# Hash attention by whole pairs: scores of both query halves in one phase, hashes, values and sums in another

## Chip, cores, metric

One core of a Trainium2 chip runs the kernel. The metric is the device time of one execution in microseconds (us), median over runs. Ratios are the mean time of one kernel's runs over the mean of the other's runs of the same rounds, so they are not quite the ratio of the medians that stand beside them.

## The reference

```python
def _attn_ref(q, k, v, proj):              # 4 x 8 heads, 768 tokens, head size 64
    q_bucket = sum(((q @ proj) > 0) * 2**arange(6))      # k_bucket likewise
    mask = q_bucket[:, :, :, None] == k_bucket[:, :, None, :]
    scores = where(mask, q @ k.T / 8, -1e9)
    attn = exp(scores - max) / (sum + 1e-9)
    return attn @ v
def _moe_ref(x, w_in, w_out):              # 3072 x 512, 512 x 2048, 2048 x 512
    h = x @ w_in
    return (h * sigmoid(1.702 * h)) @ w_out
```

The attention's output, laid out as 3072 x 512, is the input of the second block. All is float32. The change touches the attention stage alone, about the first 325 us.

## The kernel before

Attention goes over 16 pairs of heads (n = 0 to 15). The 768 queries of a pair are two halves (c = 0, 1). For each half and each of six key tiles TensorE computes scores into PSUM, ScalarE takes the exponential into SBUF (`es[c]`), GpSimd adds the exponentials of tiles 0 to 2 (`add_low`), VectorE those of tiles 3 to 5 and GpSimd's result (`add_high`), and TensorE multiplies all six with the values. Around this lie the hashes of the next pair, the row totals `dn` of the pair before, and the normalization. VectorE also converts a piece of `w_in` per pair, in the steps of `convert`.

The lines are shortened, and the loop is shown as it runs for pairs 1 to 15.

```python
def turn(n, name):                         # qT or kT of pair n: a VectorE transpose (L391)
    nc.vector.transpose(xt, x)
def hashed(n):                             # TensorE, L408: k and q, both halves, four column tiles
def featured(n):                           # VectorE f (L413), then 8 small DMAs to feats
def add_low(n, c):                         # GpSimd, L440 and L441
    acc = accs[n, c, 0] = st.tile(..., tag="acc0", bufs=1)
    nc.gpsimd.tensor_tensor(acc, es[c][:, 0], es[c][:, 1], op=Alu.add)
    nc.gpsimd.tensor_tensor(acc, acc, es[c][:, 2], op=Alu.add)
def add_high(n, c):                        # VectorE, L446, L448, L448
    nc.vector.scalar_tensor_tensor(acc, e[0], T * TINY, e[1], op0=Alu.add, op1=Alu.add)
    for x in (e[2], accs.pop((n, c, 0))):
        nc.vector.tensor_tensor(acc, acc, x, op=Alu.add)
def total(n):                              # TensorE, L479: dn, in PSUM pool mps
def invert(n):                             # VectorE: rt from dn, reciprocals r, rs
def norm(n):                               # VectorE, L499: xT times rs, two SBUF inputs
... (cut)
for g in range(len(groups) + 2):           # a group is one half (n, c)
    scores(n, c, kts); add_low(n, c)
    if hashes: featured(hashes.pop())
    if ended: add_high(*prev[:2])          # prev is the group before
    ... (turn k, norm, total of the pair before, turn q, invert)
    values(*prev); unload(*prev[:2])
    if "q" in turned: hashed(n + 1); fetch(n + 2, "k"); fetch(n + 2, "q"); fetch_v(n + 1)
    step(n, 3)                             # three conversion steps
```

So TensorE's order in a pair is scores, dn, values, hashes, scores, values: a half's values run one group after its scores.

## Time and profile before

| | kernel before |
|---|---|
| time, median | 878.85 us (878.79 to 879.34) |
| TensorE busy | 99% of the span |
| VectorE busy | 82% of the span; in attention 0.75 us idle per pair |
| one pair of attention | 19.53 us (the last two that can be counted: 19.99 and 19.97) |
| granted TensorE clock, mean (1 is full speed) | 0.997 |

The page and the chain that ended last tell what bounds the kernel; the chain in order of time shows of what a pair consists; the timelines of VectorE and GpSimd show what happens beside it. The lines are in the prediction.

### The profile page before, as it was taken

How to read it: one execution, taken by the hardware profiler on the slowest of the kernel's cores; microseconds unless marked ns; L12 is line 12 of the kernel's file. 1: busy time of each engine (PE TensorE's matmuls, PEld its weight loads, DVE VectorE, ACT ScalarE, POOL GpSimd, SP SyncE). 2: the span in 40 equal slices, each digit the busy share in tenths (PEclk: the TensorE clock that was granted, in tenths of full speed). 3: DMA queues.
4: the chain of work that ended last, by engine and by line, in shares of the span. 5: the costliest groups of instructions: out<-in, count | busy, mean ns of one | idle time of the engine just before them, and what ended most of it. 6: DMA issues, size and time to landing. Idle time of an engine off the chain costs nothing.

```text
span 877.2 us, 11895 instructions
## 1 busy us (share of the span) xinstructions
PE 866.8 (99%) x4077; PEld 498.4 (57%) x4077; DVE 723.3 (82%) x1020; ACT 314.8 (36%) x519; POOL 323.7 (37%) x275
## 2 busy tenths in 40 slices
PE   9999999999999999999999999999999999999996
PEld 5444444444444444444444444444888888888885
DVE  4589989999999986787777887888897977897786
ACT  5766776677666642223232223322000000000000
POOL 4343343333433364675433444559903100000000
PEclk9999999999999999999999999999999999999998
DMA  5544545665544203555455545575845685477524
GB/s 131 94 63 82 106 83 93 100 99 91 83 83 85 67 1 133 203 204 192 160 195 208 201 164 199 184 250 179 309 155 182 188 230 210 157 221 241 192 96 100
DMA packets 169157, 132.01 MB, mean 150 GB/s; under 512 B 123616, under 2 KB 138112, under 8 KB 163712
## 3 DMA queue, kind: packets, MB, share of 16 engines
q1 hardware_dynamic: 166528, 129.70, 52.1%
q10 hardware_dynamic: 2560, 1.46, 0.7%
q8 instruction: 34, 0.56, 0.3%
q14 instruction: 35, 0.29, 0.1%
HBM read 79.69 MB, written 50.33 MB: 148 GB/s over the span
## 4 chain that ended last, share of the span: by engine, by line
PE 97%; DVE 2%; DMA 0%; issue 0%; ACTq 0%; ACT 0%; DVEq 0%
PE product L708 33%; PE product L820 27%; PE ps L432 18%; PE av L458 15%; PE dn L479 2%; PE hash L408 1%; DVE xT L824 1%; PE tp L366 1%; DVE y L800 1%; DMA k<-in_k_dram 0%; PE hash L373 0%; DVE v L824 0%; DVE t2a L221 0%; DVE raw_g L220 0%; ACTq L807 0%
## 5 line engine op out<-in xcount | busy, mean ns | idle before, releaser
L433 ACT ACTIVATE e<-ps 128x768 f32<-128x768 f32 x192 | 151.2, 812 | 15.0 <-PE ps L432 12.7
L432 PE MATMUL ps<-qT,kT 64*128 64x384 f32 x768 | 155.1, 482 | 0.0
L708 PE MATMUL product<-xT,w_in_sb 128*128 128x512 f32 x288 | 135.5, 593 | 0.0
L458 PE MATMUL av<-e,v 128*64 128x385 f32 x768 | 131.5, 490 | 0.0
L440 POOL TENSOR_TENSOR acc<-e 128x768 f32<-128x768 f32 x32 | 58.7, 1835 | 192.5 <-DVE acc L448 130.1
L716 ACT ACTIVATE c<-c 128x512 f32<-128x512 f32 x72 | 45.4, 630 | 186.8 <-issue 78.9
L458 PEld LDWEIGHTS av<-e,v 128*64 128x64 f32 x768 | 52.2, 136 | 76.4 <-issue 75.9
L708 PEld LDWEIGHTS product<-xT,w_in_sb 128*128 128x128 f32 x288 | 54.6, 190 | 69.2 <-issue 64.1
L708 PE MATMUL product<-t_x,s_in 128*128 128x512 f32 x192 | 90.2, 592 | 0.0
L432 PEld LDWEIGHTS ps<-qT,kT 64*128 64x128 f32 x768 | 68.1, 188 | 35.4 <-issue 35.3
L219 POOL TENSOR_TENSOR v<-c,u 128x512 f32<-128x512 f32 x24 | 34.2, 1425 | 123.2 <-ACT c L716 123.2
L833 ACT COPY u<-product 128x256 f32<-128x256 f32 x21 | 7.8, 373 | 172.1 <-PE product L820 138.9
L432 PE MATMUL ps<-qf,kf 64*128 64x384 bf16 x384 | 62.9, 324 | 0.1
L708 PEld LDWEIGHTS product<-t_x,s_in 128*128 128x128 f32 x192 | 36.5, 190 | 45.9 <-issue 43.8
L441 POOL TENSOR_TENSOR acc<-acc,e 128x768 f32<-128x768 f32 x32 | 59.1, 1847 | 2.5
L708 PE MATMUL product<-xT,s_in 128*128 128x512 f32 x96 | 45.1, 592 | 0.0
L708 PE MATMUL product<-t_x,w_in_sb 128*128 128x512 f32 x96 | 45.1, 592 | 0.0
L432 PEld LDWEIGHTS <-kf 64*128 64x128 bf16 x384 | 18.9, 94 | 41.3 <-issue 19.5
L446 DVE SCALAR_TENSOR_TENSOR acc<-e 128x768 f32<-128x768 f32 x32 | 32.2, 1007 | 5.1 <-ACT e L433 5.1
L469 ACT COPY vs<-av 128x1 f32<-128x1 f32 x32 | 5.1, 159 | 86.1 <-PE av L458 86.1
L820 PE MATMUL product<-raw_g,xT 128*128 128x256 f32 x152 | 35.1, 379 | 0.0
L448 DVE TENSOR_TENSOR acc<-acc,e 128x768 f32<-128x768 f32 x32 | 32.3, 1009 | 3.3
(207 smaller groups left out, 1546.3 us busy)
## 6 DMA issues: line engine op xcount, KB each, us to landing
raw_g<-g_dram SPq DMA_DIRECT2D x22, 1024.0 KB
s_in<-g_dram SPq DMA_DIRECT2D x20, 1024.0 KB
g_dram<-c SPq DMA_DIRECT2D x72, 256.0 KB
g_dram<-t SPq DMA_DIRECT2D x48, 256.0 KB
raw<-in_moe_w_in_dram SPq DMA_DIRECT2D x16, 512.0 KB
raw<-in_moe_w_out_dram SPq DMA_DIRECT2D x16, 512.0 KB
v<-in_v_dram SPq DMA_DIRECT2D x32, 192.0 KB
g_dram<-u SPq DMA_DIRECT2D x24, 256.0 KB
```

The source lines that it names most:

```text
L219: return [lambda: eng.tensor_tensor(t1, b12, b11, op=Alu.subtract), lambda: eng.tensor_tensor(b12, b22, b12, op=Alu.subtract), lambda: eng ...
L432: nc.tensor.matmul(ps[:, j, 0:HS], a[hs, keys], m[hs, cols], start=not last, stop=last)
L433: nc.scalar.activation(es[c][:, kt, :, 0:HS], ps[:, :, 0:HS], Act.Exp, scale=1.0 / D**0.5)
L440: nc.gpsimd.tensor_tensor(acc, es[c][:, 0, :, 0:HS], es[c][:, 1, :, 0:HS], op=Alu.add)
L441: nc.gpsimd.tensor_tensor(acc, acc, es[c][:, 2, :, 0:HS], op=Alu.add)
L446: nc.vector.scalar_tensor_tensor(acc, e[0], T * TINY, e[1], op0=Alu.add, op1=Alu.add)
L448: nc.vector.tensor_tensor(acc, acc, x, op=Alu.add)
L458: nc.tensor.matmul(av[D * j : D * (j + 1), :], vt[:, t, j, :], es[c][:, t, j, :], start=(t == 0), stop=(t == T - 1))
L479: nc.tensor.matmul(dn[r0 : r0 + 32, :], ones[:, 0:32], acc[:, j, :], start=True, stop=True)
L708: nc.tensor.matmul(ps, wq[LEFT[i]][:, kc, :], xq[RIGHT[i]][:, kc, :], start=(kc == 0), stop=(kc == K2 - 1))
L716: nc.scalar.activation(c, c, Act.Gelu_apprx_sigmoid)
L820: nc.tensor.matmul(ps, wq[LEFT[i]][:, c, :], gq[RIGHT[i]][:, c, :], start=(c == 0), stop=(c == F4 - 1))
```

## The change

The intent: run both halves' scores in one go and both halves' values in one go, so that TensorE changes its tile shape less often. The loop over groups becomes a loop over pairs. The core of the diff (pairs 1 to 15; pair 0 is written out, and is much as before):

```diff
-pool, tag = (mps, "m") if (n, c) == (last, 1) else (aps, "av")
+pool, tag = (mps, "m") if c else (aps, "av")
-dn = accs[n] = mps.tile([P, HS], F32, tag="m", name="dn")
+dn = accs[n] = aps.tile([P, HS], F32, tag="av", name="dn")
-for g in range(len(groups) + 2):
-    ... (cut)
+for n in range(1, last + 1):
+    scores(n, 0, every)
+    add_low(n, 0)
+    if n == 1:
+        add_high(0, 1)
+        turn(2, "k")
+        total(0)
+    invert(n - 1)
+    norm(n - 1)
+    if 1 < n < last:
+        turn(n + 1, "k")
+    scores(n, 1, every)
+    add_low(n, 1)
+    add_high(n, 0)
+    if n < last:
+        turn(n + 1, "q")
+        hashed(n + 1)
+        featured(n + 1)
+        ... (measure; in the last pair two guards instead)
+    step(n, 2)
+    add_high(n, 1)
+    values(n, 0, every)
+    unload(n, 0)
+    step(n, 4)
+    values(n, 1, every)
+    unload(n, 1)
+    total(n)
+    ... (fetches of n + 2, conversion and sums)
```

More of the change, by code (lines that the diff above doesn't have):

```diff
@@ L485, in invert @@
                 nc.vector.transpose(rt.rearrange("p s i -> p (s i)"), accs.pop(n))
-                yield
                 r = st.tile([P, 2, HS // 32], F32, tag="r", name="r")
@@ L499, in norm @@
                 nc.vector.tensor_tensor(x, x, rs.rearrange("p (t s) -> p t s", t=T), op=Alu.mult)
-            groups = [(n, c, kts) for n in range(len(pairs)) for c in range(2)
-                      for kts in ((range(GT), range(GT, T)) if n == 0 else (range(T),))]
             last = len(pairs) - 1
@@ L525, in guard @@
                     nc.vector.tensor_reduce(largest[0:1, 0:1], row, axis=AX.X, op=Alu.max)
-            totals, norms, hashes = [], [], []
+            low, high, every = range(GT), range(GT, T), range(T)
             rest = first_pair()
@@ L532, in attention @@
                 fetch(1, x)
-            for g in range(len(groups) + 2):
-                n, c, kts = groups[g] if g < len(groups) else (last + 1, 0, ())
-                prev = groups[g - 1] if 1 <= g <= len(groups) else None
-                if kts:
-                    scores(n, c, kts)
-                    if g == 0:
-                        rest()
-                    if kts[0] == 0:
-                        add_low(n, c)
-                if hashes:
-                    featured(hashes.pop())
-                ended = prev and prev[2][-1] == T - 1
-                if ended:
-                    add_high(*prev[:2])
-                    if prev[1] == 1:
-                        totals.append((g + (g == len(groups)), prev[0]))
-                turned = ("", "k", "q", "")[g] if n == 0 else "kq" if c == 0 and n < last else ""
-                inverted = iter(())
-                for x in turned[:1]:
-                    turn(n + 1, x)
-                    measure(n + 1, x)
-                while norms:
-                    norm(norms.pop(0))
-                if totals and totals[0][0] == g:
-                    norms.append(totals.pop(0)[1])
-                    total(norms[-1])
-                    inverted = invert(norms[-1])
-                    next(inverted)
-                for x in turned[1:]:
-                    turn(n + 1, x)
-                    measure(n + 1, x)
-                whole(inverted)
-                if prev:
-                    values(*prev)
-                if ended:
-                    unload(*prev[:2])
-                if "q" in turned:
-                    hashed(n + 1)
-                    if n:
-                        hashes.append(n + 1)
-                    else:
-                        featured(n + 1)
-                    for x in "kq" if n else "q":
-                        if n + 2 <= last:
-                            fetch(n + 2, x)
-                    fetch_v(n + 1)
-                elif turned:
-                    fetch(n + 2, turned)
-                if kts and kts[-1] == T - 1:
-                    step(n, 3)
-                    if c == 0 and n > last - len(x_sums):
-                        x_sums[n - last - 1]()
-                    if c == 1:
-                        begin(n + 1)
-                if g in (len(groups) - 3, len(groups) - 2):
-                    guard(g - len(groups) + 3)
-                if g == len(groups):
-                    for f in in_sums(0):
-                        f()
-                    early.close()
-                    next(ff)
@@ L598, in attention @@
-            for x in norms:
-                norm(x)
+            scores(0, 0, low)
+            rest()
+            add_low(0, 0)
+            scores(0, 0, high)
+            turn(1, "k")
+            measure(1, "k")
+            values(0, 0, low)
+            fetch(2, "k")
+            scores(0, 1, low)
+            add_low(0, 1)
+            add_high(0, 0)
+            turn(1, "q")
+            measure(1, "q")
+            values(0, 0, high)
+            unload(0, 0)
+            hashed(1)
+            featured(1)
@@ new lines, in attention @@
+            fetch(2, "q")
+            fetch_v(1)
+            scores(0, 1, high)
+            values(0, 1, low)
+            values(0, 1, high)
+            unload(0, 1)
+            for n in range(1, last + 1):
[14 more added lines that the diff above has]
+                    turn(n + 1, "q")
+                    hashed(n + 1)
+                    featured(n + 1)
+                    for x in "kq":
+                        measure(n + 1, x)
+                else:
+                    guard(0)
+                    guard(1)
+                step(n, 2)
[6 more added lines that the diff above has]
+                total(n)
+                if n + 2 <= last:
+                    for x in "kq":
+                        fetch(n + 2, x)
+                if n < last:
+                    fetch_v(n + 1)
+                    begin(n + 1)
+                if n > last - len(x_sums):
+                    x_sums[n - last - 1]()
@@ L602, in shifted_attention @@
+            for f in in_sums(0):
+                f()
+            early.close()
+            next(ff)
+            invert(last)
+            norm(last)
     def shifted_attention():
```

## The prediction

> **What bounds the kernel now.** I read the page first: engine totals, then the chain that ended last.
>
> ```profile
> PE 866.8 (99%) x4077; PEld 498.4 (57%) x4077; DVE 723.3 (82%) x1020; ACT 314.8 (36%) x519; POOL 323.7 (37%) x275
> PE 97%; DVE 2%; DMA 0%; issue 0%; ACTq 0%; ACT 0%; DVEq 0%
> ```
>
> TensorE is never idle for long and is itself the end of the chain. So only two things can move the time: TensorE work that vanishes, and waits put where there are none. The change touches only the attention stage (to about 325 us); the feed-forward stage that follows keeps its program. Next I read one pair of that stage in the chain in order of time (start, us, what).
>
> ```profile
> 183.39 4.95 PE ps L432 x36
> 188.34 0.78 PE dn L479 x8
> 189.13 4.03 PE av L458 x24
> 193.16 0.78 PE hash L408 x8
> 193.94 4.95 PE ps L432 x36
> 198.89 4.03 PE av L458 x24
> 202.93 4.95 PE ps L432 x36
> ```
>
> One pair is scores of a half (ps), row totals (dn), values (av), hashes, scores of the other half, values: 2 x 4.95 + 2 x 4.03 + 2 x 0.78 = 19.52 us. Between its starts lies nothing but TensorE. Inside a run of scores one key tile takes 0.806 us, so six are 4.84 us, and the remaining 0.11 us of the 4.95 is the change to another shape. A value run is twelve steps of 0.3225 us, 3.87 us, plus 0.16 us for the change. The timelines of VectorE (DVE) and GpSimd (POOL) over the same pair are the third view.
>
> ```profile
> 197.43 0.96 DVE L448 TENSOR_TENSOR acc<-acc,acc 128x768 f32<-128x768 f32 x1
> 198.31 0.95 DVE L499 TENSOR_TENSOR xT<-xT,rs 128x768 f32<-128x768 f32 x1
> 199.18 2.03 DVE L193 SCALAR_TENSOR_TENSOR w_in_sb<-raw,w_in_sb 128x512 f32<-128x512 uint32 x1
> 201.25 2.05 DVE L195 TENSOR_TENSOR w_in_sb<-bits,w_in_sb 128x512 f32<-128x512 f32 x1
> ...
> 187.69 1.54 POOL L440 TENSOR_TENSOR acc<-e 128x768 f32<-128x768 f32 x1 [4.48 <-ACT e L433]
> 189.31 1.69 POOL L441 TENSOR_TENSOR acc<-acc,e 128x768 f32<-128x768 f32 x1
> 198.54 2.12 POOL L440 TENSOR_TENSOR acc<-e 128x768 f32<-128x768 f32 x1 [7.53 <-DVE acc L448]
> 200.74 2.01 POOL L441 TENSOR_TENSOR acc<-acc,e 128x768 f32<-128x768 f32 x1
> ```
>
> VectorE is nearly full too: from 75 to 255 us its only idle time per 19.53 us pair is 0.75 us, waiting for dn. The two conversions of L193 and L195 take 2.0 us each here, and POOL's pair of adds takes 2.12 + 2.01 us where it takes 1.54 + 1.69 us beside VectorE transposes (187.69). The instructions of line L193, minimum, median and maximum in ns, show that this is not its own cost:
>
> ```profile
> L193 DVE SCALAR_TENSOR_TENSOR part<-raw,part x18: 695/696/696, 352.9 to 581.2; 128x512 f32<-128x512 uint32 x18
> L193 DVE SCALAR_TENSOR_TENSOR w_in_sb<-raw,w_in_sb x14: 2031/2034/2036, 62.4 to 317.8; 128x512 f32<-128x512 uint32 x14
> ```
>
> **What the Trainium skill says.** First, SBUF — State Buffer, "Who interferes with whom": a VectorE instruction with two SBUF inputs and a GpSimd instruction that reads SBUF share a port pair, and the later one "fully blocks" until the earlier ends. The trace agrees closely: POOL's L440 starts at 198.54, is held by L499 until 199.1 and ends at 200.66; L193 ends 0.55 us after that, at 201.21; L441 then ends 1.54 us after L193; L195 ends 0.55 us after L441. So a waiting pair of instructions runs strictly in turn. Second, TensorEngine Tiling (Array Packing), "Key Properties": changing the tiling mode drains TensorE. The trace agrees: 0.11 us leaving scores (64 rows), about 0.16 us leaving values. Third, TensorE: Matmul & The Clock Gate, "What's actually happening": about 3.4 us of idle halves the clock; no trace here shows such a gap, and I use it only to judge a gap of 2.7 us below.
>
> **Removed.** The new pair is twelve key tiles of scores, hashes, both values runs together, dn. Scores: 12 x 0.806 + 0.11 = 9.78 us. Hashes 0.78. Both values runs back to back occur once now, at the end of attention, and there the next product starts 7.92 us after their start:
>
> ```profile
> 316.88 7.99 PE L458 MATMUL av<-e,v 128*64 128x385 f32 x48
> ```
>
> dn 0.78. Sum 19.26 us, so two mode changes fewer save 0.26 us per pair, 3.9 us over 15 pairs. This is the most that the change can gain. No instruction is dropped on any engine. PSUM serves: dn takes the bank of the first values run, which is unloaded 4 us earlier. ScalarE's exponentials are spaced 0.80 us against TensorE's 0.806, so three score buffers suffice for twelve tiles in a row.
>
> **Added: the hashes now wait for VectorE.** Today hashes of the next pair stand behind dn and values, and the transpose qT they need is done 2.5 us before them (190.64 against 193.16). Now they stand right behind the scores, at 9.78 us after the pair's start, and in VectorE's order before qT come: rt, the reciprocals and rs (from dn), the normalization L499, kT, and the three adds of the first half (L446, L448, L448). I walk it, time 0 at the start of a pair's scores. In pair 0 the second half's scores start at 18.96 and POOL's first add at 21.69, thus at 2.73:
>
> ```profile
> 18.96 0.34 PE L432 MATMUL ps<-qf,kf 64*128 64x384 bf16 x2
> ...
> 21.69 1.55 POOL L440 TENSOR_TENSOR acc<-e 128x768 f32<-128x768 f32 x1 [4.69 <-ACT e L433]
> ```
>
> rt starts at 0.13 (0.91 after dn starts, as at 189.19), and 0.58 + 0.30 + 0.95 + 0.98 us of single-input work less overlaps brings L499 to 2.79. L440 has the port until 4.27. L499 then ends 0.81 later (0.95 less its 0.14 start-up), at 5.08. L441 ends 1.54 later, at 6.62, with kT beside it. L446 (its tiles are ready at 5.1) ends 0.81 later, at 7.43. The two L448 take 0.10 + 0.96 each: 9.55. qT starts 0.08 before that and takes 0.96: 10.43. Hashes at about 10.53, where TensorE was free at 9.78: a wait of 0.75 us per pair. If L499 gets the port first, the same adds in another order give 10.4, so the figure doesn't hang on who wins.
>
> Pair: 19.26 + 0.75 = 20.01 us. From 46.58 to 301.43 the present kernel does 13 pairs, 19.60 us each (the last few carry a 1.2 us sum more on VectorE). +0.41 x 13 = +5.3 us.
>
> Does VectorE then keep up? After the hashes: 0.91 until f, f 0.59, L178 held by POOL's second add (9.6 to 12.9) until 13.45, L182 0.73, three adds 3.0, then L186, L193, L195, L198 free of POOL, 0.66 + 0.70 + 0.72 + 0.65: done at about 19.9. The next rt is due at 20.1. So it just keeps up, and up to 1.4 us of lateness would be swallowed at L499, which waits for the port until 4.27 anyway. That also covers the 1.2 us sums in pairs 12 to 15.
>
> **The start.** Pair 1 alone still has dn of pair 0 between its halves. VectorE must do rt to L499 after it (dn ends at 36.65, L499 at 40.3), then three adds (43.3) and qT (44.25); hashes at 44.35 against a free TensorE at 41.6: a wait of 2.7 us, under the 3.4 us of the page named, so I assume full clock. Pair 2 then starts at 53.8. Now it starts at 46.58 with 4.81 us of pair 1 left, 51.39. +2.4 us. **The end.** Pair 15 has no hashes, but its dn may wait 0.5 us, because the early weight sums on POOL then compete with the adds; against it one saving: -0.15 us.
>
> Sum +2.4 + 5.3 - 0.15 = +7.5 us: 886.4.
>
> **Rivals.** (1) Pure gain: qT is in time, time 875 to 878. For it: only 0.75 us is missing, and mode changes are certain to go. Against: L446 can't start before the port is free, whichever order. (2) VectorE becomes the bound: if L193 and L195 stay at 2.0 us, VectorE ends at 22.6 instead of 19.9, L499 starts 2.5 late, qT ends near 11.6, and a pair takes 21.2 us: +21 us, about 902. For it: VectorE has 0.75 us to spare per pair today, and the new order adds idle time around the hashes (about 1 us). Against: POOL's adds, as walked, are over before L193. (3) The k tiles come late: the queue now sends the eight feature copies (6.5 us) first, then k, which lands 3.8 us after its first issue (190.05 to about 193.9 by the DMA share in half-microsecond windows): about 2.6 us into the next pair. kT is due after L499, so 1 us or more to spare; if not, +0.5 us a pair, 893.
>
> **Range and chances.** Main case 886.4. Each 0.1 us of error in the hash wait is 1.4 us, and the walk is good to some 0.3 us: 882 to 891. With a part of rivals (1) and (3): 879 to 894. The 2% limits are 861 and 896.4. Faster by 2% is out of reach of a 3.9 us saving; slower needs rival (2) or lateness that builds up.
>
> **What will tell.** Right: values x48 of 7.9 us per pair; hashes preceded by about 0.7 us of idle TensorE, released by DVE qT; pair spacing near 20.0 us; L193 back at 0.7 us; L499 near 2 us. Wrong: pair spacing 19.3 (no wait), or above 20.5 (VectorE-bound, dn or scores waiting, L193 still 2 us), or kT waiting for a DMA.

## The result

The changed kernel takes 888.67 us, median of six runs (886.31 to 889.01), against 878.82 us of the kernel before in the same rounds: ratio 1.0107, 95% interval 1.0094 to 1.012. It is 9.8 us slower; 886.4 was forecast, in a range of 879 to 894.

In the changed kernel the normalization is L498; the other attention lines keep their numbers. The page of the changed kernel, engine totals and chain:

```profile
PE 873.2 (98%) x4077; PEld 502.7 (57%) x4077; DVE 722.4 (81%) x1020; ACT 313.9 (35%) x519; POOL 319.0 (36%) x275
PE 94%; DVE 4%; issue 1%; DMA 0%; ACTq 0%; DVEq 0%; ACT 0%
```

The instructions are as many as before. VectorE has now a share of 4% in the chain, where it had 2%. One pair in the chain in order of time (start, us, what):

```profile
196.36 9.80 PE ps L432 x72
206.15 1.49 PE hash L408 x8
207.64 7.92 PE av L458 x48
215.56 0.78 PE dn L479 x8
```

Against the prediction's lines of before: scores 9.80 us, where two runs took 9.90; values 7.92, where two took 8.06; dn 0.78 as before; hashes 1.49, where they took 0.78. So 0.24 us are saved and 0.71 lost per pair. The timelines of VectorE and GpSimd in the same pair show why the hashes are late:

```profile
199.41 1.96 DVE L498 TENSOR_TENSOR xT<-xT,rs 128x768 f32<-128x768 f32 x1
201.29 0.96 DVE L391 STREAM_TRANSPOSE kT<-k 128x768 f32<-128x768 f32 x1
202.19 1.54 DVE L446 SCALAR_TENSOR_TENSOR acc<-e 128x768 f32<-128x768 f32 x1
205.78 0.97 DVE L391 STREAM_TRANSPOSE qT<-q 128x768 f32<-128x768 f32 x1
...
199.02 1.54 POOL L440 TENSOR_TENSOR acc<-e 128x768 f32<-128x768 f32 x1 [9.69 <-ACT e L433]
200.63 2.29 POOL L441 TENSOR_TENSOR acc<-acc,e 128x768 f32<-128x768 f32 x1
```

L498 (0.95 us in the kernel before) starts during GpSimd's L440 and ends 0.8 us after it; GpSimd's L441 ends 1.55 us after L498; L446 ends 0.8 us after L441; and qT ends at 206.75, 0.6 us after the hashes' turn at 206.15. TensorE isn't idle in that time: it runs the hashes of k, which together with those of q would have cost almost nothing (0.78 us for both), and then those of q alone.

From dn to dn most pairs take 19.98 us. Pair 5 alone takes 20.35: VectorE sat idle for 0.46 us ahead of its second L448 there. What it waited for isn't shown; e2 and e11 have the same pair of 20.33 and 20.34 us, and e4 hasn't.

Pair 1 is a case of its own. The timelines of TensorE and VectorE there, and the clock of TensorE in half-microsecond windows (window, length, busy and instructions of TensorE, then of weight loads, VectorE, ScalarE and GpSimd, then the granted clock, DMA share and GB/s):

```profile
41.41 0.84 PE L408 MATMUL hash<-kT,pf_k 128*32 128x384 f32 x4
45.06 1.49 PE L408 MATMUL hash<-qT,pf_q 128*32 128x384 f32 x4 [2.82 <-DVE qT L391]
46.49 8.83 PE L458 MATMUL av<-e,v 128*64 128x385 f32 x48
39.59 1.56 DVE L498 TENSOR_TENSOR xT<-xT,rs 128x768 f32<-128x768 f32 x1
...
44.00:44.50 0.50, 0.00 (x0) 0.00 (x0) 0.50 (x2) 0.13 (x2) 0.23 (x1) 1.00 0.00 0
44.50:45.00 0.50, 0.00 (x0) 0.00 (x0) 0.50 (x1) 0.00 (x0) 0.50 (x1) 0.82 0.00 0
45.00:45.50 0.50, 0.43 (x2) 0.19 (x4) 0.01 (x1) 0.00 (x0) 0.50 (x1) 0.50 0.00 0
48.00:48.50 0.50, 0.50 (x6) 0.21 (x4) 0.40 (x2) 0.00 (x0) 0.00 (x0) 0.77 0.00 0
48.50:49.00 0.50, 0.50 (x6) 0.14 (x2) 0.50 (x1) 0.00 (x0) 0.00 (x0) 1.00 0.08 19
```

TensorE is idle for 2.82 us, and near the end of it the granted clock falls to 0.5, from about 44.8 to 48.2 us. The hashes of q take 1.49 us there (0.84 elsewhere), and the values 8.83 us (7.99 elsewhere). The normalization L498 takes 1.56 us here although GpSimd is idle from 36.75 to 44.27, so this is no wait for the port. It is 1.56 to 1.60 us in the kernel before and in every version looked at, and pair 0, whose output it treats, is the one pair that `x_of` in the kernel walks in another order; that the order is the reason wasn't tested.

### The profile page after: what moved, and what is told of

It is laid out like the page before. It is cut to its first block, busy times and chain, and to the rows that moved or that the text cites. A ratio compares the mean times of both kernels' runs of the same rounds, so it can differ in the third digit from the quotient of the medians. Undisturbed runs are those within 1.5% of the kernel's fastest.

```text
span 886.9 us, 11860 instructions
## 1 busy us (share of the span) xinstructions
PE 873.2 (98%) x4077; PEld 502.7 (57%) x4077; DVE 722.4 (81%) x1020; ACT 313.9 (35%) x519; POOL 319.0 (36%) x275
## 4 chain that ended last, share of the span: by engine, by line
PE 94%; DVE 4%; issue 1%; DMA 0%; ACTq 0%; DVEq 0%; ACT 0%
PE product L705 33%; PE product L817 27%; PE ps L432 16%; PE av L458 14%; PE hash L408 2%; PE dn L479 1%; DVE xT L821 1%; PE tp L366 1%; DVE y L797 1%; DVE acc L448 0%; DVE acc L446 0%; DMA k<-in_k_dram 0%; PE hash L373 0%; DVE rs L493 0%; DVE qT L391 0%
## 5 line engine op out<-in xcount | busy, mean ns | idle before, releaser
L458 PE MATMUL av<-e,v 128*64 128x385 f32 x768 | 129.1, 491 | 0.0
L440 POOL TENSOR_TENSOR acc<-e 128x768 f32<-128x768 f32 x32 | 49.3, 1541 | 206.6 <-ACT e L433 155.5
L458 PEld LDWEIGHTS av<-e,v 128*64 128x64 f32 x768 | 54.0, 136 | 74.1 <-issue 70.7
L441 POOL TENSOR_TENSOR acc<-acc,e 128x768 f32<-128x768 f32 x32 | 62.7, 1960 | 2.5
L446 DVE SCALAR_TENSOR_TENSOR acc<-e 128x768 f32<-128x768 f32 x32 | 40.3, 1261 | 5.1 <-ACT e L433 5.1
L448 DVE TENSOR_TENSOR acc<-acc,acc 128x768 f32<-128x768 f32 x32 | 31.0, 969 | 3.7 <-DVE acc L448 0.5
```

The source lines that it names most:

```text
L440: nc.gpsimd.tensor_tensor(acc, es[c][:, 0, :, 0:HS], es[c][:, 1, :, 0:HS], op=Alu.add)
L441: nc.gpsimd.tensor_tensor(acc, acc, es[c][:, 2, :, 0:HS], op=Alu.add)
L458: nc.tensor.matmul(av[D * j : D * (j + 1), :], vt[:, t, j, :], es[c][:, t, j, :], start=(t == 0), stop=(t == T - 1))
```

## The experiments

The theory: the changed kernel loses 0.71 us in each of pairs 2 to 14 because qT stands behind work that GpSimd's hold on the shared port stretches, and loses some 5 us in pair 1 by the idle gap and the low clock after it; the two savings of tile-shape changes are real and hidden below that. Rivals: VectorE is the bound as a whole; tiles land too late; the savings aren't real; the low clock has another cause. "Changed" below is the changed kernel at 888.67. Spacings are from one dn to the next in TensorE's timeline.

### e1: qT early, pairs 2 to 14

```diff
                 if 1 < n < last:
                     turn(n + 1, "k")
+                    turn(n + 1, "q")
                 scores(n, 1, every)
...
-                    turn(n + 1, "q")
+                    if n == 1:
+                        turn(n + 1, "q")
```

> Edit: the transpose of the next pair's queries (qT) goes ahead of the first half's adds on VectorE, in pairs 2 to 14 only. Theory A (the whole steady loss is the hashes waiting 0.71 us per pair for qT, which sits behind those adds): pair spacing 19.98 -> 19.27 us, hash q directly behind hash k, -0.71 x 13 = -9.2 us against the changed kernel: about 879.4 us. Rival B (VectorE as a whole is the bound, so order on it doesn't matter): spacing stays near 20.0 us, about 888.5. Rival C (the q tiles land too late to turn earlier): qT waits for a DMA, gain under half, 884 or more.

Measured: 883.25 us (ratio to the kernel before 1.0037, 1.0023 to 1.0051), 5.4 us off the changed kernel where 9.2 were expected. The six runs fall in two groups, 880.15 and 880.26 us, and 883.15 to 884.61; the granted clock doesn't tell them apart (0.995 and 0.996 against 0.996 and 0.997), and only a run of the slower group (884.61) was profiled, so what follows is shown for that group, and what the two faster runs had is open. The hashes are on time, as theory A says. But the spacing is 19.28 us for three pairs only, then 19.70. In the chain of e1, and in VectorE's timeline of an earlier pair:

```profile
222.66 0.78 PE hash L408 x8
231.36 1.21 PE dn L479 x8
...
119.22 1.92 DVE L498 TENSOR_TENSOR xT<-xT,rs 128x768 f32<-128x768 f32 x1
126.36 1.73 DVE L178 SCALAR_TENSOR_TENSOR w_in_sb<-raw,mask_3fffffff 128x512 uint32<-128x512 uint32 x1
128.12 2.05 DVE L182 SCALAR_TENSOR_TENSOR bits<-raw,w_in_sb 128x512 uint32<-128x512 uint32 x1
```

Now dn takes 1.21 us, 0.43 more than the 0.78 of the changed kernel. VectorE has no idle time left: L498, L178 and L182 are stretched by 1.0, 1.05 and 1.35 us over the 0.95, 0.68 and 0.69 that they take beside an idle GpSimd (L178 and L182 in e7), 3.4 us in all, where the changed kernel has 1.0 + 0.6 (L446) + 0.9 (L178) = 2.5. It falls behind for three pairs and then delays dn in each. So theory A holds for the wait of the changed kernel, and in the profiled run rival B holds for what comes behind it: one wait was replaced by a smaller one.

### e2: qT early, pair 1 alone

```diff
                     turn(2, "k")
+                    turn(2, "q")
                     total(0)
...
-                    turn(n + 1, "q")
+                    if n > 1:
+                        turn(n + 1, "q")
```

> Edit: the same, in pair 1 alone. Theory: the idle gap of 2.8 us there vanishes and with it the spell of granted clock 0.5 (44.5 to 48.4 us), which costs hash q 0.7 us and the values 0.84 us: -2.8 -1.5 = -4.3 us against the changed kernel, about 884.4; PE clock 1.00 throughout 40 to 52 us. Rival (the clock spell has another cause than the gap): -2.8 only, about 885.9, with the clock still 0.5 near 45 us.

Measured: 883.18 us (1.005, 1.0037 to 1.0063), 5.5 us off. The clock is 1.00 in all windows from 41 to 50 us. The theory holds, and its size was too small by 1.2 us: the hashes of pair 1 go from 5.08 us (41.41 to 46.49) to 0.78, which is 4.30 us and not 2.8 + 0.7, because the k hashes had run alone before the gap; with 0.84 us of values it is 5.1, and the rest, 0.4 us, is within the intervals of the two ratios.

### e3: both

> Edit: both of these. If the two losses are independent, -9.2 - 4.3 = -13.5 us against the changed kernel: about 875.1 us, 0.4% below the kernel before (878.8): then the 0.26 us per pair of mode changes saved shows at last. Rival (the savings of mode changes are not real): 878 to 879.

Measured: 881.1 us (1.0025, 1.0012 to 1.0038), where 875.1 was expected. Spacing 19.70 us, as in e1, and reached from pair 3 on; that it comes sooner because VectorE has no rest in pair 1 without the gap is argued only. The dn of pair 2 lost a further 1.0 us: in that pair kT waits 0.59 us and qT 1.91 us for their tiles to land, and dn then waits for VectorE. The two edits aren't independent. The rival, that the savings aren't real, is not shown by this: the wait for dn hides them.

### e4: the gap filled with useless matmuls

```diff
                     turn(n + 1, "q")
+                    if n == 1:
+                        for _ in range(12):
+                            nc.tensor.matmul(aps.tile([P, 512], F32, tag="av", name="fill"), idle[:, 0:P], idle, ...)
                     hashed(n + 1)
```

> Edit: the changed kernel with 12 useless bf16 matmuls on a zero tile[...] ahead of the hashes of pair 1, so that TensorE is busy while it waits for qT. Theory (idle gap lowers the granted clock): the wait stays, clock stays 1.00, values x48 take 7.92 us instead of 8.76: -1.5 us against the changed kernel, about 887.1, and no run-to-run jump of 2.4 us. Rival (the low clock has nothing to do with the gap): clock still 0.5 near 45 us, 888.7 or, if the fill delays the hashes, more.

Measured: 888.07 us in four runs (887.77 to 888.43; 1.0103, 1.0089 to 1.0118). TensorE's timeline, and one clock window of the kind above:

```profile
41.73 5.14 PE L570 MATMUL fill<-idle 128*128 128x512 bf16 x12
47.58 7.99 PE L458 MATMUL av<-e,v 128*64 128x385 f32 x48
...
45.00:46.00 1.00, 0.89 (x3) 0.19 (x2) 0.35 (x1) 0.00 (x0) 1.00 (x1) 1.00 0.68 108
```

The wait stays, the clock stays 1.00 and the values take 7.99 us again: without the idle gap the clock isn't lowered. The profiles of all versions fit this, and show that such a gap doesn't always do it. Between 36 and 66 us the clock falls below 1.00 in five of the six that have the gap of 2.8 us in pair 1 (the changed kernel, e1, e5, e7, e11; not e6), and in none of the eight that don't have it. The gain is 0.6 us, not 1.5, because my fill was too long: 12 matmuls of 0.43 us each, 5.14 us, for an idle gap of 2.8 us, so the hashes came later than in the changed kernel (46.80 against 45.06; 1.4 us later when both are counted from the dn of pair 0, at 35.99 and 35.67).

### e5: GpSimd's first two adds left out (wrong result)

```diff
             def add_low(n, c):
+                if n > 1 and c == 0:
+                    return
...
-                for x in (e[2], accs.pop((n, c, 0))):
+                for x in (e[2], es[c][:, 0, :, 0:HS] if n > 1 and c == 0 else accs.pop((n, c, 0))):
```

> Wrong result on purpose: from pair 2 on GpSimd's two adds of the first half are left out (the totals lack two tiles); every VectorE instruction stays, with the same sizes. Theory A (qT is late because GpSimd holds the shared port ahead of L498 and L446): L498 1.96 -> 0.95 us, L446 of the first half 1.54 -> 0.95 us, qT ends about 1.3 us earlier, no wait before the hashes, spacing 19.27 us: about 879.4 us. Rival B (VectorE's own order suffices for the wait, the port matters little): L498 and L446 get shorter but the wait stays above 0.4 us and the time above 884.

Measured: 879.4 us, as expected (1.0003, 0.9987 to 1.002); the result is wrong, as meant. From VectorE's timeline and from the chain (L500 is the normalization, L448 the first of the three adds):

```profile
214.76 0.96 DVE L500 TENSOR_TENSOR xT<-xT,rs 128x768 f32<-128x768 f32 x1
216.74 0.96 DVE L448 SCALAR_TENSOR_TENSOR acc<-e 128x768 f32<-128x768 f32 x1
...
221.50 0.78 PE hash L408 x8
```

The normalization takes 0.96 us, the hashes 0.78, the spacing is 19.27 to 19.28 us in all pairs from 2 to 14. VectorE's order alone doesn't make qT late; GpSimd's adds beside it do. The edit also takes away that the last of VectorE's adds needs GpSimd's sum, but in the changed kernel that sum is ready at 202.92, 2.0 us before the add that reads it, so this isn't what qT waited for. That the time fits so well is in part luck: in the profiled run (880.04) the low clock in pair 1 lasted 6.8 us instead of 3.4 and dn came 21.12 us after the dn before instead of 19.58, while the stray 0.37 us of pair 5 and the 0.3 us that the last dn waits are gone. With nothing waiting, the spacing is 0.25 us under the 19.53 of the kernel before, so the savings of shape changes are real too.

### e6: normalization late

```diff
-                norm(n - 1)
+                if n in (1, last):
+                    norm(n - 1)
...
                     featured(n + 1)
                     ... (measure)
+                    if n > 1:
+                        norm(n - 1)
```

> Edit: the normalization (L498) of the pair before goes behind the hashes' feature step, off the way to qT, in pairs 2 to 14; qT stays behind the adds. By the walk: GpSimd's adds then run 2.7 to 5.9 us without L498 between them, L446 waits for the port until 5.9, ends 6.7, two adds 8.8, qT 9.7: the hashes' wait falls from 0.71 to about 0.05 us, spacing 19.3 us, about 880. Rival (L498 is only in the queue, its place doesn't matter as VectorE is the bound): 888.

Measured: 879.67 us (1.0014, 0.9998 to 1.0031), 9.0 us off. Hashes 0.89 us, spacing 19.38. The walk of the prediction, redone for another order, gave 0.05 us of wait; it is 0.11. The rival is out. This kernel still has the gap in pair 1, and its four runs fall in two groups by the mean granted clock: 878.40 and 879.10 us at 0.998, 880.23 and 880.72 at 0.996. In the profiled one (878.40) the gap is 2.83 us long and the clock stays 1.00.

### e7: every qT twice

```diff
-                nc.vector.transpose(xt, ...)
+                for _ in range(2 if name == "q" and n > 2 else 1):
+                    nc.vector.transpose(xt, ...)
```

> Edit: the changed kernel with every qT from pair 3 on transposed twice, 12 extra VectorE instructions of 0.87 us spacing, right ahead of the hashes. Theory A (TensorE waits for qT each pair, with no slack): +0.87 x 12 = +10.5 us, about 899. Rival (slack somewhere else in the pair swallows it): under +3 us.

Measured: 901.2 us (1.0253, 1.0236 to 1.027), +12.5. The spacing goes from 19.98 to 21.00 us, as two transposes in a row are 1.0 us apart and not 0.87, and there are 13 extra ones, pairs 3 to 15, and not 12. So there is no slack at this place: what VectorE does ahead of qT is paid for in full.

### e8: dn beside the hashes

Built on e3: `total(n - 1)` moves right ahead of `hashed(n + 1)`, rt right behind it, the normalization behind f, and GpSimd and VectorE add into one tile of three buffers.

```diff
+                if n > 1:
+                    total(n - 1)
+                    add_low(n, 1)
+                    inverted = invert(n - 1)
                 if n < last:
                     hashed(n + 1)
+                next(inverted, None)
...
-                total(n)
+                if n == last:
+                    total(n)
```

> A step further, built on both early transposes: the totals of the pair before (dn) stand right before the hashes, which have the same tile shape, so one more mode change per pair goes; GpSimd's adds go into the same tile as VectorE's (room for a third set of sums). Theory (a mode change between different tile shapes costs about 0.14 us): spacing 19.27 -> 19.13 us, -1.8 us against e3, about 873.3. Rival (values of the first half wait for the bank that dn leaves, or feature copies come late): no gain or slower than e3, with an idle TensorE before av or ps.

Measured: 887.48 us (1.0097, 1.008 to 1.0114), a miss. The steady spacing is 19.29 us: the hashes start 0.66 us after dn and not 0.78, so a shape change is saved, but the values start 0.92 us after the hashes and not 0.78, because their bank is free only when rt has read dn. The rest of the loss is in edges of my own making: waits of 0.87, 4.88 and 3.10 us in pairs 1, 2 and 15, two of them with a low clock behind them. It doesn't settle what dn beside the hashes could bring.

### e9, e10 and the changed kernel again

e9 is e6 with the edit of e2. e10 is e3 with the normalization behind the first half's adds:

```diff
                 invert(n - 1)
-                norm(n - 1)
...
                 add_high(n, 0)
+                norm(n - 1)
```

> Edit: the late normalization (e6) together with the early query transpose in pair 1 (e2). If the two repairs are independent (-9.0 and -5.5 us measured apart against the changed kernel's 888.7): about 874.2 us, faster than the kernel before by 0.5%. If they share a cause or VectorE fills up again, as it did when both query transposes were moved ahead: 877 or more. Spacing 19.38 us, no granted clock below 1.00 between 40 and 60 us.

> Edit: both query transposes early (e3), and the normalization moved behind the first half's adds, so that GpSimd's first two adds meet no VectorE instruction with two SBUF inputs. Theory (e3's wait of 0.43 us before dn came from VectorE being full with waits for the shared port: L498 1.92, L178 1.73, L182 2.05 us): at least one of the three falls to its free length, VectorE gets idle time, neither the hashes nor dn wait, spacing 19.27 us, 1.4 us under e9: about 872.8. Rival (moving the waits only moves them: L498 now meets GpSimd's second pair of adds): spacing 19.5 or more, 876 or more.

> The changed kernel unchanged, beside e9 and e10 on one chip. If the spell of low clock in pair 1 depends on where the idle gap falls, most runs are at 888.7 with a mean clock of 0.995 and a few near 886.3 with 0.997, as among the first six; if 886.3 was a chance of another kind, all are at 888.7.

Measured on one chip, before at 878.85: e9 875.57 us (0.9965, 0.9952 to 0.9979), e10 875.79 (0.9967, 0.9954 to 0.9981), the changed kernel 888.71 (1.0111, 1.0096 to 1.0126), its four runs at 888.03 to 889.29 with clocks 0.995 and 0.996. e9 is a version that beats both kernels, 13.1 us under the changed one, where the two repairs alone gave 9.0 + 5.5; they add up but for 1.4 us. In e10 the spacing becomes 19.28 us as the theory says, with L498 at 0.95 us. But its time is 3 us above my 872.8: pairs 2 and 3 together take 2.5 us more than twice that. VectorE's and TensorE's timelines:

```profile
59.84 0.98 DVE L391 STREAM_TRANSPOSE qT<-q 128x768 f32<-128x768 f32 x1 [2.08 <-DMA q<-in_q_dram]
...
71.74 0.84 PE L479 MATMUL dn<-acc,ones 128*32 128x384 f32 x4 [1.34 <-DVE acc L448]
```

There the early transpose waits 2.08 us for its tiles, and dn then waits for VectorE. In the later pairs it waits for them too, 0.37 to 1.23 us, without cost to TensorE. So rival C of e1 isn't out: without waits for the port, the landing of the tiles is the next thing that an early qT meets. As for e11: no run showed the fast group this time, so one run of ten (886.31 us, clock 0.997) is in it; e6 shows the two groups better.

### e12: as e10, but pair 2 with qT behind the adds

```diff
                     turn(n + 1, "k")
-                    turn(n + 1, "q")
+                    if n > 2:
+                        turn(n + 1, "q")
...
                 add_high(n, 0)
+                if n == 2:
+                    turn(n + 1, "q")
                 norm(n - 1)
```

> Edit: as e10, but pair 2 keeps the query transpose behind the first half's adds, because there e10's transpose waited 2.1 us for its query tiles to land and dn then waited 1.3 us for VectorE; e10 lost 2.5 us in pairs 2 and 3 against its later spacing of 19.28 us. Theory (that is all that e10 lost): about 2.4 us under e10's 875.8, 873.4 us, 0.6% under the kernel before, the fastest version. Rival (the loss moves to pair 3, whose tiles also land late): 875 or more.

Measured: 875.38 us (0.9954, 0.9941 to 0.9968), 0.4 us under e10 and not 2.4. In pair 2 now kT waits 2.86 us for its tiles to land, and in pair 3 kT waits 1.19 and qT 1.93 us; the rival was right. e9, e10 and e12 lie within their intervals of each other. Fetching earlier in these pairs wasn't tried.

## Why the prediction was right

It was right in direction and in mechanism; one step, the start, failed, in two assumptions: full clock behind the gap, and the length of one normalization.

- **What bounds the kernel.** TensorE's order, with nothing to gain but shape changes: shown by e5, where no wait is left in the steady pairs. The pair's pieces were forecast as 9.78, 0.78, 7.92, 0.78 and measured as 9.80, 0.78, 7.92, 0.78 there; in the changed kernel the hashes take 1.49.
- **The hashes' wait.** Forecast 0.75 us per pair, measured 0.71; spacing 20.01 forecast, and from the dn of pair 1 to that of pair 14 it is (315.52 - 55.25) / 13 = 20.02 us. (Most pairs have 19.98; that the mean comes so near is luck, as the stray 0.37 us of pair 5 is in it.) That GpSimd's adds, and not VectorE's order alone, make it, is shown by e5; that they do it through the port is read from the trace, where each of the instructions in question ends a fixed time after the other engine's; that it has no slack, by e7; that moving one instruction out of it removes it, by e6. In one point the picture was wrong: TensorE isn't idle in the wait, it runs the k hashes alone.
- **VectorE keeps up.** Right for the changed kernel: the next rt follows L198 at 196.42 without delaying scores. Rival (2) was wrong in its form, since L193 did return to 0.69 us, but e1 shows how near it is: with qT early, other instructions meet GpSimd and VectorE becomes the bound.
- **Late k tiles, rival (3).** Not in the changed kernel's steady pairs. In e3, e10 and e12 late k and q tiles cost time in pairs 2 and 3.
- **The start.** The step that failed. Forecast: a wait of 2.7 us at full clock, because 2.7 is under 3.4, +2.4 us in all. Measured: the hashes' turn came at 41.41 and those of q started at 45.06, 3.65 us later. That the idle gap in it, 2.82 us, looks like the forecast 2.7 is luck, as the k hashes filled the rest; and then came half clock. The first scores of pair 2 start at 56.03 and not at 53.8: 0.7 us because qT came later (its hashes at 45.06, not 44.35), 0.65 us of slow q hashes and 0.84 us of slow values. qT came later mainly because the walk gave the normalization of pair 0 the usual 0.95 us, where it takes 1.56; the kernel before shows 1.57 at 42.21. This is nearly all of the difference between the forecast 886.4 and the measured 888.7. e2 shows that without the gap clock and time return, e4 that a filled gap keeps the clock.
- **The end.** Forecast a wait of dn in pair 15 of 0.5 us; it took 1.14 us for the usual 0.85, so 0.3.

The intended gain, 0.24 us in each pair, was there all the time and was outweighed by a new wait and by the gap with the low clock in pair 1. With both repaired (e9) the order by whole pairs is 0.35% faster than the kernel before.

## What to carry to other kernels

When work on the bounding engine is regrouped, list for each of its phases what the other engines must have done by then, in their own order, and walk that list with the stretched durations: an instruction's slack can vanish though no instruction is added. Where VectorE and GpSimd met on the shared port they ran in turn, so an instruction in another's window can take two or three times its own length (0.95 us became 1.96, and in e1 0.69 became 2.05), and the waiting shows as the instruction's own duration. And look at every idle gap of a matrix engine of some microseconds, even one that comes once: here the slow clock behind a gap of 2.82 us cost 1.5 us more.

## What the Trainium skill lacked or had wrong

- TensorE: Matmul & The Clock Gate, "What's actually happening", says that at least one idle window of about 3.4 us takes the clock to half. Here an idle gap of 2.82 us (changed kernel, pair 1) was enough, with the clock at 0.5 from about 44.8 to 48.2 us, 3.4 us in all; a gap of 2.83 us in e6's profiled run left it at 1.00. So gaps somewhat shorter than the window can trip it, in some executions and not in others, and 3.4 us isn't a safe limit. In e5 the spell behind a gap of 2.84 us lasted 6.8 us.
- TensorEngine Tiling (Array Packing), "Key Properties", says that a change of tiling mode drains TensorE, and gives no time. Here a change took 0.11 us when leaving the scores and 0.16 us when leaving the values, by the sums of the prediction; the pairs with one change fewer of each kind save 0.10 and 0.14 us (9.80 for 9.90, 7.92 for 8.06). That all of this is the drain isn't shown.
- SBUF — State Buffer, "Who interferes with whom", fits every meeting of VectorE and GpSimd that was followed here (the kernel before, the changed one, e1 and e6) to about 0.1 us. It doesn't say that the profile counts the blocked time as the instruction's own: the normalization shows 1.96 us instead of 0.95, and the conversion L193 shows 2.03 us in the kernel before and 0.69 in the changed one.
- No page looked at says what a late operand costs among column tiles that run together: the hashes of k and q take 0.78 us when both are ready and 1.49 us when q comes 0.7 us late.
